# Parallel sliding attention and bilinear GLU on one core: the first weight loads regrouped, one load moved ahead of a transposing DMA, one input load on another queue, the last chunk's logits in one group

## The chip, the cores and the metric

One core of a Trainium2 chip runs the whole kernel. The metric is the device time of one execution in microseconds (us); the runs' median stands for a kernel. Engines are named as in the profile: PE multiplies matrices (PEld loads its weights), DVE works on vectors, ACT applies functions and copies, POOL does small vector work, SP only issues DMAs. ACT and POOL can issue DMAs too.

## What is computed

All tensors are bf16; there are S = 2048 positions of D = 640 numbers, 32 heads of 20, and F = 1536. No layer norm has a gain or bias.

```python
    xn = _layernorm(x)                                   # over the 640 numbers of a position
    q, k, v = split(xn @ wqkv)                           # 32 heads of 20
    idx = pos[:, None] - 2 * arange(8)                   # 8 keys per position: 0, 2, .. 14 back
    logits = where(idx >= 0, einsum("bhsd,bhswd->bhsw", q, k[idx]) * 20 ** -0.5, -1e9)
    o = einsum("bhsw,bhswd->bhsd", softmax(logits), v[idx]) @ wo
    g, u = xn @ w_gate, xn @ w_up
    out = x + o + (g * u) @ w_down
```

## The kernel before

**Tiles and chunks.** The 2048 positions are 16 tiles of 128 positions; four tiles are a chunk of 512 positions, and there are four chunks, 0 to 3. A layer-normed tile is transposed (features on partitions), into `xnT` of its chunk. Tiles 0 to 2 are transposed by PE (L385) and copied by ACT (L390), in the pieces of `PIECES`; tiles 3 to 15 by a transposing DMA that SP issues (L379).

**What a chunk goes through.** `proj` (L500) makes q, k and v of a chunk, 25 matmuls of 128x512 each, evicted by ACT (L504). For chunk 0 it is done in parts, as its tiles come: `proj_tile` (L464, evicted at L477) makes q for tiles 0, 1 and 2 one by one, then `proj` makes k for those three tiles at once, then `proj_tile` makes q and k for tile 3, then `proj` makes v of the chunk. The 8 logits of a position and head are products on DVE (L555), folded there in three steps (L530 twice, L535) and summed over the last numbers of a head by PE with the 0/1 matrix `Ek` (L582) into the PSUM tile `pl`. DVE and ACT make the softmax (L618 the largest, L622, ACT L632 the exponential, L640 the sum, L643 the reciprocal, L649 the result `a`). `a` goes to DRAM (`aD`, L658) and comes back spread over partitions in four DMAs (`aE`, L666). DVE multiplies `aE` with v (L698), adds up in a tree (L708 twice, L706) and has `oT` of a tile. The GLU is 12 steps f of five matmuls with `w_gate` and five with `w_up` (L746), both evicted by ACT (L751), multiplied by DVE into `hT` (L763). Last, `down` multiplies `hT` with `w_down` (L809) and `oT` with `wo` (L812), 34 matmuls of 128x320 a tile, in two halves.

**What sets the order.** Work is a list of steps with engine, cost, dependencies. `Plan.order` places them in a simulated time, on each engine the most urgent of those that are ready, and the instructions are then issued in that order; each engine runs its own in order. `floor` is the planned landing of a load, `PACE` scales the planned cost of DVE's steps, and `GR` says for each chunk in how many groups the logits and the softmax are made; before, chunk 3 has two groups of four matmuls of `pl`, the others one group of eight. The logits' steps are `urgent`: they go first when ready, with a margin of 1 us behind the last fold in the planned time. PE has six banks of PSUM for all else (`ring`), so it can run some steps ahead of ACT's evictions.

**The start (L238 to L240, L879 to L920).** ACT issues three loads for `wq`, of one, two and two of its five blocks of 128 rows (L203), and then x of tile 3 (L179). SP issues x of tiles 0, 1 and 2, then `wk` (L185), then x of tiles 4, 5, 6 and 7, each of which waits for the buffer of the tile five before it (there are five). Then it issues tile 3's transposing DMA, the load of `wv`, and the transposing DMAs of tiles 4 to 7, each behind the layer norm of its tile. Then come `wg`, x of tiles 9 to 12, `wu`, `wd` and `wo`. x of tile 8 is issued by POOL (L412): it needs tile 3's buffer, so it waits for tile 3's transposing DMA, and behind it in POOL's order stand the reciprocal square roots (`rstd`, L267) of tiles 5, 6 and 7, each of which DVE needs to apply the layer norm to its tile (L272). ACT uses x of tile 8 first when it takes the mean of its rows (L326).

Of the kernel before, what the change touches and what calls it, by code (L numbers as in the profile page):

```python
# [9 lines left out]
ACT = mybir.ActivationFunctionType  # L10
# [22 lines left out]
class Plan:  # L33
# [1 line left out]

    LAG = 0.06
    RAW = 0.116
    PACE = {"DVE": 1.03, "ACT": 1.0}
    INORDER = ("DVE", "PE", "ACT")

    def __init__(self):
# [2 lines left out]
    def add(self, eng, cost, fn, deps=(), occ=None, after=(), kb=0):  # L44
        k = self.PACE.get(eng, 1.0)
        s = Step(eng, cost * k, fn, deps, None if occ is None else occ * k, after)
        s.kb = kb
        s.pace = k
        s.idx = len(self.steps)
        self.steps.append(s)  # L50
        return s
# [60 lines left out]
def kernel(  # L112
# [11 lines left out]
    nc = tc.nc  # L124
# [3 lines left out]
    S, D = x_flat.shape  # L128
# [8 lines left out]
    KT = D // P  # L137
    FT = F // P
    NT = S // P
# [16 lines left out]
    wv = const.tile([P, KT, D], BF, name="wv")  # L156
# [10 lines left out]
    add = plan.add  # L167
    T = {}

    def new(key, shape, dtype, tag, bufs, pool=None):  # L170
        t = (pool or sb).tile(shape, dtype, name=tag, tag=tag, bufs=bufs)
        T[key] = t
        return t


    def load_x(t, eng=None):
        def fn():
            x = new(("x", t), [P, D], BF, "x", 5)
            (eng or nc.sync).dma_start(out=x[:], in_=x_flat[t * P : (t + 1) * P, :])  # L179
        return fn  # L180

    X = {}

    def wload(dst, src, eng=None):
        return lambda: (eng or nc.sync).dma_start(out=dst[:], in_=src.rearrange("(i p) f -> p i f", p=P))  # L185
# [10 lines left out]
    def load(at, fn, deps=()):  # L196
        s = chain[0] = add("SP", 2.0, fn, deps, occ=0.45, after=[chain[0]])
        s.floor = at
        return s

    def part(r, lo, hi):
        src = A_wqkv[lo * P : hi * P, r * D : (r + 1) * D].rearrange("(i p) f -> p i f", p=P)
        return lambda: nc.scalar.dma_start(out=WT[r][:, lo:hi, :], in_=src)  # L203
# [29 lines left out]

    C0 = add("POOL", 0.6, consts0)
    WP = []
    for lo, hi, at in ((0, 1, 4.4), (1, 3, 5.1), (3, KT, 5.5)):
        WP.append(add("ACT", at, part(0, lo, hi), [C0], occ=0.48, after=WP[-1:]))
    X[3] = add("ACT", 5.2, load_x(3, nc.scalar), occ=0.45, after=[WP[2]])  # L238
    TB = add("ACT", 1.6, table, after=[X[3]])

    def warm():
# [38 lines left out]
    def behind(s, a):  # L280
        s.after.append(a)
        s.deps.append(a)
        plan.steps.remove(s)
        plan.steps.append(s)
# [5 lines left out]
    def st_in(t, g, d=None):  # L290
        return inline("DVE", 0.48, ln_stats(t, g), [d or X[t]], 0.395)
# [5 lines left out]
    def apply_in(t):  # L297
        XT[t] = inline("DVE", 0.443, ln_apply(t), [RS[t]], 0.4)
# [57 lines left out]
    def pe_main(cost, fn, deps=(), banks=1):  # L356
        nonlocal main
        waits = []
        for k in range(banks):
            if len(ring) + k >= 6:  # L360
                waits.append(ring[len(ring) + k - 6])
        main = add("PE", cost + 0.165, fn, [main, *waits, *deps], occ=cost)
        return main
# [6 lines left out]
    def transposes(t):  # L370
        c, q = divmod(t, CH)

        def slot():
            if q == 0:
                new(("xnT", c), [P, KT, CS], BF, "xnT", XB)

        def dma():
            slot()
            nc.sync.dma_start_transpose(out=T["xnT", c][:, :, q * P : (q + 1) * P], in_=T["x", t][:])  # L379

        def piece(g0, g1, n):
            def pe():
                ps = new(("pst", t, n), [P, KT, P], BF, "ps", 6, psum)
                for g in range(g0, g1):
                    nc.tensor.transpose(ps[:, g, :], T["x", t][:, g * P : (g + 1) * P], ident[:])  # L385

            def ev():
                if n == 0:
                    slot()
                nc.scalar.copy(T["xnT", c][:, g0:g1, q * P : (q + 1) * P], T["pst", t, n][:, g0:g1, :])  # L390
            return pe, ev

        if t in PIECES:
            for n, (g0, g1) in enumerate(PIECES[t]):
                p, e = piece(g0, g1, n)
                w = g1 - g0
                a = pe_main(w * 0.056, p, [XT.get((t, n), XT[t])])
                a = add("ACT", 0.16 + w * P / 1200, e, [a, TT.get(t)], occ=0.07 + w * P / 1200)
                TT[t] = a
                TX.setdefault(t, []).append((g0, g1, a))  # L400
                ring.append(a)
            if t:
                behind(PV[t - 1][0], TT[t])
        else:
            if c < 2:
                a = TT[t] = chain[0] = add("SP", 3.0, dma, [XT[t]], occ=1.28, after=[chain[0]])
            else:
                a = TT[t] = add("SP", 2.8, dma, [XT[t], GP.get(c - XB)], occ=1.28, kb=200)
        if t + 5 < W:
            X[t + 5] = load((11.0, 11.5, 14.2)[t], load_x(t + 5), [a])  # L410
        elif t == 3 or 8 <= t < NT - 5:
            X[t + 5] = add("POOL", 6.0, load_x(t + 5, nc.gpsimd), [a], occ=0.45, kb=160)  # L412

    LL = {}
    GR = (1, 1, 1, 2)
    PV = {}
    R = {}
    PROJ = ("q", "k", "v")
# [12 lines left out]
    def halo(c, r):  # L431
# [10 lines left out]
        else:  # L442
            w = LL.get((c - 2, GR[c - 2] - 1)) if r == 1 else O16.get(CH * (c - 1) - 1)
            HALOCP[r, c] = add("ACT", 0.25, fn, [w, *R[r, c - 1]])

    def lhs(r, i, j):
        return WT[r][:, i, :].rearrange("p (c b) -> p c b", b=KT)[:, :, j]
# [7 lines left out]
    def tile_part(r, t, n, g0, g1, deps):  # L455
        c, q = divmod(t, CH)
        j0, j1 = JS[n]

        def pe():
            if g0 == 0:  # L460
                new(("psv", r, t, n), [P, 512], F32, "ps", 6, psum)
            for j in range(j0, j1):
                for i in range(g0, g1):
                    nc.tensor.matmul(T["psv", r, t, n][:, (j - j0) * P : (j - j0 + 1) * P], lhsT=lhs(r, i, j),  # L464
                                     rhs=T["xnT", c][:, i, q * P : (q + 1) * P], start=(i == 0 and j == j0), stop=(i == KT - 1),
                                     skip_group_check=True)

        ws = WQ[: (1, 2, 2, 3, 3)[g1 - 1]] if r == 0 else WW[r]
        return pe_main((g1 - g0) * (j1 - j0) * 0.056, pe, [*deps, *ws], banks=1 if g0 == 0 else 0)

    def tile_evict(r, t, n, a):
        c, q = divmod(t, CH)
        j0, j1 = JS[n]
        w = j1 - j0

        def ev():
            nc.scalar.copy(where(r, c, j0, j1, q * P, P),  # L477
                           T["psv", r, t, n][:, 0 : w * P].rearrange("p (j s) -> p j s", s=P))

        e = add("ACT", 0.16 + w * P / 1200, ev, [a, HALOCP.get((r, c))], occ=0.07 + w * P / 1200)  # L480
        ring.append(e)
        PV.setdefault(t, []).append(e)
        R.setdefault((r, c), []).append(e)
        TO[e.idx] = q * P
# [8 lines left out]
    def proj(c, r, lo=0, n=CS):  # L493
        for j in range(KT):
# [11 lines left out]
            ts = range(c * CH + lo // P, c * CH + (lo + n) // P)  # L506
            old = LL.get((c - 2, GR[c - 2] - 1)) if r < 2 else O16.get(CH * (c - 1) - 1)
            a = pe_main(KT * (n / 2400 + 0.0027), pe, [*WW[r], *[TT[t] for t in ts], old])
# [55 lines left out]
    before = {}  # L564
    order = [(c, g) for c in range(NCH) for g in range(GR[c])]
    for a, b in zip(order, order[1:]):
        before[b] = a

    def logits(c, g):
        n = (c, g)  # L570
        E = CS // 4 // GR[c]

        def lg():
            if g == 0:
                new(("lps", c), [P, 2 * CS], F32, "pl", 1, psum)
            l = T["lps", c][:, g * W * E : (g + 1) * W * E].rearrange("p (w s) -> p w s", w=W)
            sets = 3 - GR[c]
            for b in range(sets):
# [5 lines left out]

        took = 0.2 + 0.2195 * 2 / GR[c]
        folds = [FO[4 * c + u] for u in range(4) if GR[c] == 1 or u // 2 == g]
# [282 lines left out]
    WQ = WP  # L869
# [6 lines left out]
    halo(0, 1)  # L876
    halo(0, 2)
    transposes(0)
    a0 = [None, None]  # L879
    for k, (g0, g1, x) in enumerate(TX[0]):  # L880
        for n in range(2):
            if k == 2 and n == 1:
                a = st_in(2, 0, None)
                a = st_in(2, 1, a)
                apply_in(1)
                transposes(1)
                WV = None
            a0[n] = tile_part(0, 0, n, g0, g1, [x])
            if k == 2:
                tile_evict(0, 0, n, a0[n])  # L890
# [8 lines left out]
    proj_tile(0, 2, (0,))  # L899
    apply_in(3)  # L900
    transposes(3)
    WV = load(14.6, wload(wv, A_wqkv[:, 2 * D : 3 * D]))
    WW = (WP, [WK], [WV])
    proj_tile(0, 2, (1,))
    proj(0, 1, 0, 3 * P)
# [5 lines left out]
        ln(t)  # L911
        transposes(t)
    WL["g"] = load(28.5, wload(wg, B_w_gate))
    for t in range(9, 13):
        X[t] = load(30.0, load_x(t), [TT[t - 5]])
    WL["u"] = load(36.0, wload(wu, B_w_up))
    proj(0, 2)
# [68 lines left out]
```

## Time and profile before

| | us |
|---|---|
| median of 3 runs (257.4, 257.65, 259.34) | 257.65 |
| the profiled execution | 258.23 |
| its span, first to last instruction | 256.5 |
| PE busy, in 1481 matmuls | 251.8 (98%) |
| DVE busy, in 273 instructions | 223.5 (87%) |
| ACT busy, in 250 instructions | 129.1 (50%) |
| POOL busy, in 61 instructions | 41.8 (16%) |
| DMA, mean of the span | 96 GB/s |
| TensorE clock granted | 1.0 in all stages |

The chain of waits is the way back from the last instruction: at each step to what released it, or to the instruction before it on its engine. A line of the timeline has the start, the time that the group covers, engine, line, operation, tiles and count; in brackets stands the idle time before it and what ended it. The view of DMA issues names for each issuing line the engine, the count, the size of each and the median time from issue to landing; it can be asked for a stretch, so that a single DMA is seen. SPq and ACTq are the parts of SP and ACT that issue and wait. Matmuls overlap, so busy times and ends of single ones are somewhat longer than their distance.

### The profile page before, as it was taken

What the parts mean: (1) busy time and instruction counts of PE and PEld (TensorE: products, weight loads), DVE (VectorE), ACT (ScalarE), POOL (GpSimd) and SP (SyncE); (2) the same over time, 40 slices, a digit from 0 to 9 for tenths busy, and PEclk for the clock granted to TensorE, in tenths of its full rate; (3) what the DMA queues carried; (4) which work ended last, traced back from release to release, by engine and by line L of the source; (5) the groups of instructions that cost most, each with busy time, mean ns of one, the idle gap of its engine ahead of it and who ended that gap; (6) DMA issues with size and microseconds to landing.
All of it is one profiled execution on the core that took longest, in us unless ns stands there. A gap on an engine that the chain in (4) does not pass through costs nothing.

```text
span 256.5 us, 3786 instructions
## 1 busy us (share of the span) xinstructions
PE 251.8 (98%) x1481; PEld 141.4 (55%) x1481; DVE 223.5 (87%) x273; ACT 129.1 (50%) x250; POOL 41.8 (16%) x61
## 2 busy tenths in 40 slices
PE   7999999999999999999999999999999999999995
PEld 2885554444456775444455766444457754445763
DVE  5769999997999999999999999799999999994011
ACT  2656689786589164655554114545542135554100
POOL 2432000411100711004100112000293120000110
PEclk9999999999999999999999999999999999999999
DMA  6895999058500278051400132520005534000221
GB/s 216 259 192 105 399 391 335 3 152 179 157 0 3 27 95 85 7 191 44 170 0 0 17 38 27 145 88 0 0 3 127 130 31 102 23 0 3 24 27 51
DMA packets 21953, 24.65 MB, mean 96 GB/s; under 512 B 10032, under 2 KB 18352, under 8 KB 21872
## 3 DMA queue, kind: packets, MB, share of 16 engines
q1 hardware_dynamic: 18672, 17.86, 24.0%
q0 software_dynamic: 2432, 5.57, 13.5%
q10 hardware_dynamic: 832, 0.98, 1.2%
q8 instruction: 11, 0.18, 0.3%
q14 instruction: 6, 0.05, 0.1%
HBM read 18.61 MB, written 5.96 MB: 96 GB/s over the span
## 4 chain that ended last, share of the span: by engine, by line
PE 96%; DMA 2%; ACTq 0%; DVE 0%; issue 0%
PE ps L746 40%; PE ps L500 23%; PE ps L809 20%; PE ps L812 8%; PE ps L464 3%; DMA wq<-in_A_wqkv_dram 2%; PE pl L582 1%; ACTq L203 0%; PE ps L385 0%; DVE x L820 0%; DVE gs L214 0%; DVE mhalf L216 0%; DVE dm L189 0%
## 5 line engine op out<-in xcount | busy, mean ns | idle before, releaser
L746 PE MATMUL ps<-xnT,wg 128*128 128x512 bf16 x240 | 59.7, 379 | 0.0
L746 PE MATMUL ps<-xnT,wu 128*128 128x512 bf16 x240 | 59.6, 379 | 0.0
L809 PE MATMUL ps<-wd,hT 128*128 128x320 bf16 (+2 forms) x384 | 57.4, 299 | 0.0
L698 DVE TENSOR_TENSOR av<-v,aE 128x5120 bf16<-128x5120 bf16 (+1 forms) x20 | 45.6, 2286 | 3.7 <-DMA aE<-aD 3.7
L809 PEld LDWEIGHTS <-hT 128*128 128x128 bf16 x384 | 37.0, 98 | 16.3 <-issue 0.7
L555 DVE TENSOR_TENSOR pw<-qk 128x2560 bf16<-128x2560 bf16 x28 | 40.8, 1485 | 0.1
L746 PEld LDWEIGHTS <-wu 128*128 128x128 bf16 x240 | 23.5, 98 | 28.3
L746 PEld LDWEIGHTS <-wg 128*128 128x128 bf16 x240 | 23.3, 98 | 28.1 <-issue 0.5
L751 ACT CAST us<-ps 128x512 bf16<-128x512 f32 x48 | 28.1, 585 | 21.2 <-PE ps L746 20.2
L751 ACT CAST gs<-ps 128x512 bf16<-128x512 f32 x48 | 28.1, 585 | 20.4 <-PE ps L746 20.3
L708 DVE TENSOR_TENSOR av<-av 128x2560 bf16<-128x2560 bf16 (+1 forms) x32 | 36.9, 1153 | 0.2
L824 ACT COPY y<-ps 128x320 f32<-128x320 f32 x28 | 11.5, 426 | 42.6 <-PE ps L812 32.7
L853 POOL DMA_DIRECT2D out_dram<-y x14 | 12.2, 871 | 105.3 <-ACT y L824 86.7
L812 PE MATMUL ps<-wo,oT 128*128 128x320 bf16 (+2 forms) x160 | 27.0, 299 | 0.0
L504 ACT CAST qk<-ps 128x512 bf16<-128x512 f32 (+1 forms) x35 | 19.9, 569 | 12.2 <-PE ps L500 12.2
L530 DVE TENSOR_TENSOR pw<-pw 128x2048 bf16<-128x2048 bf16 (+1 forms) x28 | 25.6, 951 | 0.0
L500 PE MATMUL ps<-xnT,wv 128*128 128x512 bf16 x100 | 22.3, 379 | 0.0
L763 DVE TENSOR_TENSOR hT<-gs,us 128x512 bf16<-128x512 bf16 x48 | 19.7, 417 | 2.5 <-ACT us L751 2.3
L500 PE MATMUL ps<-xnT,wk 128*128 128x512 bf16 (+1 forms) x100 | 20.9, 366 | 0.0
L812 PEld LDWEIGHTS <-oT 128*128 128x128 bf16 x160 | 15.5, 98 | 6.3
L790 POOL COPY gate<-hT 1x1 bf16<-1x1 bf16 x4 | 10.6, 2652 | 51.2 <-DVE hT L763 51.2
L500 PEld LDWEIGHTS <-wv 128*128 128x128 bf16 x100 | 11.6, 118 | 9.7 <-issue 0.4
(67 smaller groups left out, 200.8 us busy)
## 6 DMA issues: line engine op xcount, KB each, us to landing
aE<-aD SPq DMA_DIRECT2D x12, 256.0 KB, 4.0
out_dram<-y POOLq DMA_DIRECT2D x14, 160.0 KB, 3.8
wg<-in_B_w_gate_dram SPq DMA_DIRECT2D x1, 1920.0 KB, 9.1
wu<-in_B_w_up_dram SPq DMA_DIRECT2D x1, 1920.0 KB, 13.0
wd<-in_B_w_down_dram SPq DMA_DIRECT2D x1, 1920.0 KB, 17.9
out_dram<-in_A_x_dram POOLq DMA_DIRECT2D x3, 640.0 KB, 4.2
x<-in_A_x_dram SPq DMA_DIRECT2D x11, 160.0 KB, 5.3
aE<-aD SPq DMA_DIRECT2D x8, 128.0 KB, 2.6
```

The source lines that it names most:

```text
L500: nc.tensor.matmul(T[key][:, 0:n], lhsT=lhs(r, i, j), rhs=T["xnT", c][:, i, lo : lo + n], start=(i == 0), stop=(i == KT - 1))
L504: nc.scalar.copy(where(r, c, j, j + 1, lo, n)[:, 0, :], T[key][:, 0:n])
L530: nc.vector.tensor_tensor(w[:, :, lo:hi, :], w[:, :, lo:hi, :], w[:, :, a:b, :], ALU.add)
L555: nc.vector.tensor_tensor(o, qh, kh, ALU.mult)
L698: nc.vector.tensor_tensor(o, v, w, ALU.mult)
L708: nc.vector.tensor_tensor(v[:, 0:k], v[:, 0:k], v[:, k : 2 * k], ALU.add)
L746: nc.tensor.matmul(ps[:], lhsT=(wu if r else wg)[:, i, f * P : (f + 1) * P], rhs=T["xnT", c][:, i, :], start=(i == 0), stop=(i == KT - 1))
L751: nc.scalar.copy(s[:], T[key][:])
L763: nc.vector.tensor_tensor(h[:], T["gs", c, f][:], T["us", c, f][:], ALU.mult)
L809: nc.tensor.matmul(ps, lhsT=T["hT", c, f][:, q * P : (q + 1) * P], rhs=wd[:, f, sl], start=(f == 0), stop=(f == FT - 1 and not wo_part))
L812: nc.tensor.matmul(ps, lhsT=T["oT", t][:, g, :], rhs=wo[:, g, sl], start=False, stop=(g == KT - 1 and f1 == FT))
L853: nc.gpsimd.dma_start(out=out_flat[t * P : (t + 1) * P, :], in_=T["y", t][:], accum_op=ALU.add)
```

## The change

`wq` is loaded in two DMAs, of three and two blocks, in place of three. `wv` is loaded by SP one step earlier: it stood behind tile 3's transposing DMA and stands now between the x of tile 6 and the x of tile 7. The x of tile 8 is issued by SP, after `wg` and with the x of tiles 9 to 12, and no longer by POOL. Chunk 3's logits and softmax are one group of eight matmuls, like those of the other chunks. Three planned landings and DVE's planned pace (1.03 to 1.02) are changed too.

```diff
-    PACE = {"DVE": 1.03, "ACT": 1.0}
+    PACE = {"DVE": 1.02, "ACT": 1.0}
...
-    for lo, hi, at in ((0, 1, 4.4), (1, 3, 5.1), (3, KT, 5.5)):
+    for lo, hi, at in ((0, 3, 4.6), (3, KT, 5.6)):
         WP.append(add("ACT", at, part(0, lo, hi), [C0], occ=0.48, after=WP[-1:]))
-    X[3] = add("ACT", 5.2, load_x(3, nc.scalar), occ=0.45, after=[WP[2]])
+    X[3] = add("ACT", 5.0, load_x(3, nc.scalar), occ=0.45, after=[WP[1]])
...
-        elif t == 3 or 8 <= t < NT - 5:
+        elif 8 <= t < NT - 5:
             X[t + 5] = add("POOL", 6.0, load_x(t + 5, nc.gpsimd), [a], occ=0.45, kb=160)
...
-    GR = (1, 1, 1, 2)
+    GR = (1, 1, 1, 1)
...
-        ws = WQ[: (1, 2, 2, 3, 3)[g1 - 1]] if r == 0 else WW[r]
+        ws = WQ[: 1 + (g1 > 3)] if r == 0 else WW[r]
...
                 apply_in(1)
                 transposes(1)
-                WV = None
+                WV = load(13.8, wload(wv, A_wqkv[:, 2 * D : 3 * D]))
...
     apply_in(3)
     transposes(3)
-    WV = load(14.6, wload(wv, A_wqkv[:, 2 * D : 3 * D]))
...
-    for t in range(9, 13):
+    for t in range(8, 13):
         X[t] = load(30.0, load_x(t), [TT[t - 5]])
```

The order that the plan makes of it was compared with that of before, engine by engine. PE's instructions stand in the same order up to the middle of chunk 1's `down`; from there chunk 2's eight logits matmuls come half a tile of `down` earlier (12 and 5 matmuls), chunk 3's first four (they stood after the first ten matmuls of chunk 2's GLU) are gone, and all eight of chunk 3 stand two halves of a tile before the place where the second four stood, in chunk 2's `down`. SP issues x of tile 4, 5 and 6, `wv`, x of tile 7, five transposing DMAs (tiles 3 to 7), `wg`, x of tiles 8 to 12, `wu`, `wd`, `wo`. POOL issues no load among the `rstd`. On DVE nothing changes before chunk 0's softmax. From there the order is shifted in places: in chunks 0, 1 and 2 one or several steps of the next chunk's products and folds that stood ahead of the first L698 stand behind the last L706 of the chunk, and chunk 3 has four L698 of 5120 elements where it had eight of 2560, and one set of softmax instructions in place of two.

## The prediction

> **What bounds the kernel now.** I read the page first, then the chain of waits in order of time, then SP's and DVE's timelines, and last the view of DMA issues for single stretches of the start.
>
> ```profile
> PE 251.8 (98%) x1481; PEld 141.4 (55%) x1481; DVE 223.5 (87%) x273; ACT 129.1 (50%) x250; POOL 41.8 (16%) x61
> ...
> PE 96%; DMA 2%; ACTq 0%; DVE 0%; issue 0%
> ```
>
> PE is busy for 98% of the span and is 96% of the chain, so the time is the start of PE's dense work, plus its matmuls, plus any gap put between them. Pieces of the chain (start, length, what):
>
> ```profile
> 2.17 5.82 DMA wq<-in_A_wqkv_dram
> ...
> 16.43 2.79 PE ps L464 x50
> 19.22 21.58 PE ps L500 x100
> ...
> 151.02 0.55 PE pl L582 x8
> 151.56 1.74 PE ps L809 x12
> ...
> 166.15 0.33 PE pl L582 x4
> ...
> 206.49 0.33 PE pl L582 x4
> 206.82 1.74 PE ps L809 x12
> ```
>
> The last load of wq lands at 2.17 + 5.82 = 7.99; from there the chain is PE alone, with no gap, until DVE's last step at 253.65. So the gain can only lie ahead of 8 us or in the few logits lines, while a loss can come wherever a supplier has little slack. Who has little slack? SP's timeline gives the issues, the view of DMA issues (one stretch for each line: 11 to 12.2, 12.2 to 13 with two lines, 14.4 to 14.7, 21 to 22) the time to landing in the last column:
>
> ```profile
> 11.11 1.31 SPq L379 DMA_TRANSPOSE xnT<-x  x1
> 12.48 1.92 SPq L185 DMA_DIRECT2D wv<-in_A_wqkv_dram  x1
> 14.50 8.47 SPq L379 DMA_TRANSPOSE xnT<-x  x4
> ```
>
> ```profile
> xnT<-x SPq DMA_TRANSPOSE x1, 4.4
> ...
> q8 instruction: 1, 0.02, 11.5%
> ...
> wv<-in_A_wqkv_dram SPq DMA_DIRECT2D x1, 800.0 KB, 6.4
> ...
> xnT<-x SPq DMA_TRANSPOSE x1, 5.0
> ...
> xnT<-x SPq DMA_TRANSPOSE x1, 2.6
> ```
>
> Tile 3's transpose lands at 11.11 + 4.4 = 15.5 and PE wants it at 16.27 (first L464 of tile 3 in PE's timeline): 0.75 us of slack. wv lands at 12.48 + 6.4 = 18.9, wanted at 19.06: 0.2. Tile 7's transpose lands at 21.77 + 2.6 = 24.4, wanted at 24.45: 0.1. Tile 4's, issued at 14.50 right behind wv, takes 5.0 and lands 0.6 after wv; tile 7's, with nothing ahead of it, takes 2.6: on SP's queue a transpose waits for the load issued before it.
>
> ```profile
> 17.26 0.45 DVE L272 TENSOR_SCALAR x<-x,mv,rstd 128x640 bf16<-128x640 bf16 x1 [2.18 <-POOL rstd L267]
> ...
> 39.71 1.29 DVE L535 TENSOR_TENSOR qk<-av 128x1024 bf16<-128x1024 bf16 x2
> ...
> 146.20 1.29 DVE L535 TENSOR_TENSOR qk<-pw 128x1024 bf16<-128x1024 bf16 x2
> ...
> 167.03 2.83 DVE L698 TENSOR_TENSOR av<-v,aE 128x5120 bf16<-128x5120 bf16 x1 [2.07 <-DMA aE<-aD]
> ...
> 203.08 1.28 DVE L535 TENSOR_TENSOR qk<-pw 128x1024 bf16<-128x1024 bf16 x2
> ```
>
> DVE loses 2.18 us at 15.1 because POOL's rstd stands behind the x of tile 8. Its folds end at 41.0 for chunk 0 (PE takes the logits from 40.74: no slack), at 147.5 for chunk 2 (151.02: 3.5) and at 204.4 for chunk 3's second group (206.49: 2.1).
>
> **The change part by part.** *wq in two loads.* One issue of 0.48 us goes, so the last load and x of tile 3 can land up to 0.48 earlier; the gain ends at 0.22, because tile 1's transposes on PE (8.40) need the layer norm that DVE ends at 7.69 + 0.43 = 8.12, and PE starts 0.06 after DVE at the first tile (5.74, 5.80). Against it, the first five L464 ran at 6.43, and must now wait for three blocks, which with the old second load landed at 7.2. Five matmuls at 0.056 are 0.28. Bounds -0.22 and +0.3; I take 0, since the two meet in the same stretch.
>
> *wv ahead of tile 3's transpose.* SP can issue wv after the x of tile 6 (issued at 8.87, 0.33 long), so at 9.2 and not 12.48: wv lands well before 19.06. But x of tile 7 and the transpose, issued at 10.4 and 11.1, now stand behind its 800 KB. In the first 13 us the busy slices of the DMA view move 354 to 410 GB/s, so 0.82 MB take 2.1 us. In the stretch from 12.2 to 13 an instruction fetch (q8) takes 11.5% of 16 engines for 0.8 us, which is 1.47 us of one engine; the transpose waits for the slowest engine, and the wv data adds to that. Upper bound: all 2.1 us are added, landing 15.5 + 2.1 = 17.6, PE waits 17.6 + 0.1 - 16.27 = 1.4. Lower bound: wv is done in its own 6.4 us, at 15.6; x of tile 7 takes 0.4 (0.16 MB at the same rate) and the transpose 0.6, as tile 4's behind wv: 16.6, a wait of 0.4; and if the transpose did not queue, 0. I take 1.4, since the row nearest to it is the transpose of before itself, with the same fetch on its engine. The x of tile 7 lands at about 17 and DVE wants it at about 15.8 (17.92 less 2.18); that costs DVE some 1 us of the 2.18 won below.
>
> *x of tile 8 on SP's queue.* POOL's rstd of tile 5 is free at 14.4; DVE is 1 to 2 us earlier, and tile 7's transpose, the folds of chunk 0 and wg with it. That moves nothing by itself, since none of them stalls PE now; it gives the cover that PE is not held at 24.45 and 40.74. The load is one issue of 0.47 on SP behind wg; it takes the place of the x of tile 9, which lands at 31.4, and ACT's mean wants it at 31.6. With PE 1.4 later that is covered; uncovered it would hold ACT's evictions, with six banks between them and PE. Cost 0. wu, one load later, lands near 39.2 and is wanted at 42.5. On SP's queue each step issued between tile 7's transpose and the logits' first store (53.59) shifts by that 0.47; no step there is waited for.
>
> *Chunk 3's logits as one group.* Two groups of four cost PE 0.33 each and 0.11 around each (12 L809 take 1.74 behind them and 1.63 elsewhere): 0.88. A group of eight costs 0.55 + 0.11 = 0.66. Gain 0.22. DVE saves 0.8 us of small softmax steps and 0.6 in L698 (eight of 1.484, four of 2.82), which PE doesn't see. What DVE has to keep is the place. Chunk 2's logits stand one half of a tile earlier (2.31): 148.7, and with the 1.4 from the start 150.1. Folds: before 147.5; a step of 1.13 that stood in DVE's wait of 1.68 us in chunk 0 now stands behind the L698s, and in chunk 1 a product of 1.40 does the same where there was no wait (0.2 of wait comes instead), so they end at 147.5 + 1.1 + 0.2 = 148.8: slack 1.3, kept by the late start. From there the first L698 of chunk 2 follows after two products (2.8), the largest, the difference, product and fold (4.9), sum, reciprocal and result (3.4), and a DMA trip of 7.0 (before: issued 160.04, L698 at 167.03): 18.1, so 166.9. Its four sets and twelve L763 took 192.25 - 167.03 = 25.2; then three products and the folds left, 10.3. Chunk 3's folds end at 202.4. PE wants them at 206.49 - 4.62 (two halves) - 0.44 (the first group gone) + 1.4 = 202.8. Slack 0.4: cost 0. Bounds: with chunk 1's trip of 5.0 (108.03 to 113.0) 2 us of slack; with chunk 0's of 7.9 (53.59 to 61.5) a wait of 0.5.
>
> Behind it, the softmax (7 us with the exponential) and a trip of 5 to 8 put the first L698 of chunk 3 at 215 to 218. The last L763 comes 21.6 after it (sums of the same rows), at 237 to 240; PE needs it 4.1 us into `down` (10 L809, 5 L812, and both again), at 235.1 + 1.2 + 4.1 = 240.4. Tile 15's oT comes 3 us after that and is wanted at 252. Covered. The pace only changes the planned order.
>
> Sum: 0 + 1.4 + 0 - 0.22 = +1.2 us. The profiled execution took 258.23, 1.73 over its span, and the median of the three is 0.58 less: 259.4 against that execution, 258.85 against the median, rounded 258.8.
>
> **The rivals.** *Tile 3's transpose is not held* (its slack of 0.75 and a faster wv suffice, say because the fetch falls elsewhere): only the logits and the start count, 257.65 - 0.22 and 0 to -0.22: 257.3. For it: 15 of 16 engines are free of the fetch. Against it: tile 4's 5.0.
>
> *Chunk 3's logits hold PE.* This is the case beyond +1%: the eight matmuls have to wait for the folds if DVE's first L698 of chunk 2 is later than 167.3. From there each us costs one. At the trip of 7.9 the wait is 0.5, so 259.4; for +1% (260.2) the trip would have to be 9.3, longer than any of the five in this trace, or DVE has to lose as much elsewhere, in front of the 25.2 us block. Price up to 2 us: 260.5.
>
> *PE's clock falls in the gap.* The ten warm-up matmuls of 128x512 take 4.45 us, against 1.08 for each five later: a slow clock, at the start alone; granted clock 1.0 afterwards. If the wait at 16.3 brought it back for as long, about 4.5 us at half speed would cost 2.2 us more: 261. The trace has no gap over 0.35 us after the warm-up to judge by, and behind that one (6.87 to 7.20) the clock stays. [...]
>
> **How the numbers follow.** 1% of the median is 2.6 us, about what a measurement here can tell from no change. Forecast (transpose held for 0.4 to 1.4, start up to 0.3: 257.8 to 259.2): 0.60. Transpose not held (257.0 to 257.6): 0.22. Logits hold PE (259.4 to 260.5): 0.13. Clock (260 to 262): 0.03. None of the cases is 2.6 faster; I leave 0.02 for what I don't see. Slower by over 2.6 are the clock case and half of the logits case: 0.10. Within 1%: 0.88. The range from 257.2 (the middle of the second case) to 260.2 leaves out half of the second case's lower part, the clock case and a part of the third.
>
> **What would show it.** In the timeline of the changed kernel: wv issued near 9.3; tile 3's transpose landing at 17.6 and an idle time of PE of 1.4 ended by xnT near 16.3 (the step is wrong if it lands by 16.2); no idle time of DVE for rstd near 15; the first L464 no earlier than 6.9; no PE wait at the L582 lines; a granted clock of 1.0 around 18 us. The prediction fails if a landing that I read as near to its need (x of tile 8 at ACT, wq's three blocks at PE) holds PE by over 1 us.

## The result, and the profile after

The changed kernel takes 258.43 us (median of 22 runs, 258.09 to 259.31); in the same comparison the kernel before takes 257.45 (22 runs, 257.26 to 259.34). The ratio is 1.003, 95% interval 1.0019 to 1.004, so the change costs 0.5 to 1.0 us. The profiled execution of the changed kernel took 258.12, its span is 256.3.

The page of the changed kernel: busy times, the clock granted to TensorE in 40 slices, and the shares of the chain by engine.

```profile
PE 251.6 (98%) x1481; PEld 141.7 (55%) x1481; DVE 223.5 (87%) x264; ACT 129.0 (50%) x249; POOL 41.4 (16%) x60
...
PEclk9999999999999999999999999999999999999999
...
PE 93%; DMA 3%; DVE 3%; POOL 0%; issue 0%
```

No engine has over 0.3 us more to do than before (PEld 141.7 us, before 141.4), and the clock granted is 1.0 from its first record in the trace, at 7.08, to PE's last matmul. The chain is 93% PE where it was 96%: the first 16 us of it have moved to other engines. Its pieces in the changed kernel (start, length, what):

```profile
9.13 0.07 issue
9.20 0.56 POOL rstd L267
9.76 0.03 issue
9.78 0.46 DVE x L272
10.24 0.02 issue
10.25 5.77 DMA xnT<-x
16.03 0.05 issue
16.07 2.99 PE ps L464 x50
...
148.46 0.54 PE pl L582 x8
149.00 1.74 PE ps L809 x12
...
201.19 0.54 PE pl L582 x8
201.73 1.74 PE ps L809 x12
```

PE's work now starts, for the chain, at 16.07, when tile 3's transposing DMA has landed; before, it was PE alone from 8 us on. The three logits pieces (0.55, 0.33 and 0.33) are two of 0.54, and neither has a wait. The idle time itself in PE's timeline and in that of its weight loads, same kernel:

```profile
16.07 1.59 PE L464 MATMUL ps<-xnT,wq 128*128 128x128 bf16 x25 [0.26 <-DMA xnT<-x]
```

```profile
16.07 1.44 PEld L464 LDWEIGHTS <-wq 128*128 128x128 bf16 x25 [0.63 <-DMA xnT<-x]
```

The two differ by 0.37, since the profile models the ends of matmuls; below I go by starts. SP's timeline and single stretches of the view of DMA issues (10.2 to 10.3, then 9.6 to 10) of the changed kernel give the cause:

```profile
8.63 0.43 SPq L185 DMA_DIRECT2D wv<-in_A_wqkv_dram  x1
9.77 0.33 SPq L179 DMA_DIRECT2D x<-in_A_x_dram  x1
10.25 10.26 SPq L379 DMA_TRANSPOSE xnT<-x  x5
```

```profile
xnT<-x SPq DMA_TRANSPOSE x1, 5.8
...
x<-in_A_x_dram SPq DMA_DIRECT2D x1, 160.0 KB, 5.7
```

wv is issued at 8.63 (before: 12.48), and what stands behind it is slow: x of tile 7 takes 5.7 us (before: 4.5), the transpose 5.8 (4.4). DVE's timeline of the changed kernel, next to the row of 2.18 us that the prediction showed:

```profile
15.46 0.89 DVE L253 BATCH_NORM_STATS2 st<-x 128x6 f32<-128x320 bf16 x2 [0.46 <-DMA x<-in_A_x_dram]
...
164.59 2.83 DVE L698 TENSOR_TENSOR av<-v,aE 128x5120 bf16<-128x5120 bf16 x1 [0.23 <-DMA aE<-aD]
...
198.98 1.29 DVE L535 TENSOR_TENSOR qk<-pw 128x1024 bf16<-128x1024 bf16 x2
```

The 2.18 us behind POOL's rstd are gone, 0.46 for x of tile 7 came. Chunk 3's last fold ends at 200.27 and PE takes the logits at 201.12: they fit, by 0.85.

### The profile page after: what moved, and what is told of

Its sections match the earlier page's. It is cut to its first block, busy times and chain, and to the rows that moved or that the text cites. A ratio compares the mean times of both kernels' runs of the same rounds, so it can differ in the third digit from the quotient of the medians.

```text
span 256.3 us, 3767 instructions
## 1 busy us (share of the span) xinstructions
PE 251.6 (98%) x1481; PEld 141.7 (55%) x1481; DVE 223.5 (87%) x264; ACT 129.0 (50%) x249; POOL 41.4 (16%) x60
## 4 chain that ended last, share of the span: by engine, by line
PE 93%; DMA 3%; DVE 3%; POOL 0%; issue 0%
PE ps L746 40%; PE ps L500 21%; PE ps L809 20%; PE ps L812 8%; DMA xnT<-x 2%; DVE st L253 1%; PE ps L464 1%; DMA x<-in_A_x_dram 1%; PE pl L582 1%; DVE x L272 1%; DVE ve L261 0%; DVE mv L259 0%; POOL rstd L267 0%; DVE x L820 0%
## 5 line engine op out<-in xcount | busy, mean ns | idle before, releaser
L809 PE MATMUL ps<-wd,hT 128*128 128x320 bf16 (+2 forms) x384 | 57.4, 299 | 0.0
L698 DVE TENSOR_TENSOR av<-v,aE 128x5120 bf16<-128x5120 bf16 x16 | 45.1, 2820 | 3.9 <-DMA aE<-aD 3.9
L809 PEld LDWEIGHTS <-hT 128*128 128x128 bf16 x384 | 37.0, 98 | 16.5 <-issue 0.8
L853 POOL DMA_DIRECT2D out_dram<-y x14 | 12.2, 872 | 103.8 <-ACT y L824 103.8
L504 ACT CAST qk<-ps 128x512 bf16<-128x512 f32 (+1 forms) x35 | 19.9, 568 | 11.2 <-PE ps L500 11.2
L500 PE MATMUL ps<-xnT,wv 128*128 128x512 bf16 x100 | 22.3, 379 | 0.0
L500 PE MATMUL ps<-xnT,wk 128*128 128x512 bf16 (+1 forms) x100 | 20.9, 366 | 0.0
L500 PEld LDWEIGHTS <-wv 128*128 128x128 bf16 x100 | 11.6, 117 | 9.7 <-issue 0.4
```

Source lines behind the costliest of these rows:

```text
L500: nc.tensor.matmul(T[key][:, 0:n], lhsT=lhs(r, i, j), rhs=T["xnT", c][:, i, lo : lo + n], start=(i == 0), stop=(i == KT - 1))
L504: nc.scalar.copy(where(r, c, j, j + 1, lo, n)[:, 0, :], T[key][:, 0:n])
L698: nc.vector.tensor_tensor(o, v, w, ALU.mult)
L809: nc.tensor.matmul(ps, lhsT=T["hT", c, f][:, q * P : (q + 1) * P], rhs=wd[:, f, sl], start=(f == 0), stop=(f == FT - 1 and not wo_part))
L853: nc.gpsimd.dma_start(out=out_flat[t * P : (t + 1) * P, :], in_=T["y", t][:], accum_op=ALU.add)
```

## A second profile of before

Each kernel below was timed together with the kernel before. The first two are the kernels of this case once more.

> The kernel before, unchanged: a second profile. The profile of before took 258.23 us, 0.8 over its median of 257.45, so its start may have been a slow one: there one DMA engine was about 1 us behind the other fifteen from 4.5 us on, and wq's last load landed at 7.99. If the late engine belongs to that one execution, a second profile has wq's last load at about 6.8 and a span near 255.6; if it belongs to the kernel, it is there again at 8.0. Ratio 1.000.

> The changed kernel, unchanged: a second profile. The one at hand took 258.12 us, near its fastest (258.09) and 0.3 under its median. If tile 3's transposing DMA behind wv is the loss, PE's wait for xnT is 0.4 us in the fast profile and 0.6 to 1.0 in one near the median, and there is no other gap. Ratio 1.003.

before_again: 257.45 us (257.27 to 258.67), ratio to the other runs of before 0.9986 [0.9965, 1.0007]. after_again: 258.38 (258.03 to 258.91), ratio 1.0014 [0.9995, 1.0033]. The chain of before_again shows that the start which the prediction read was not the usual one:

```profile
1.28 4.43 PE ps L244 x10
5.71 0.69 PE ps L385 x5
6.39 0.28 PE ps L464 x5
6.68 0.01 issue
6.69 1.05 PE ps L464 x16
...
15.61 2.79 PE ps L464 x50
18.40 5.61 PE ps L500 x26
```

There is no wait for wq in it: PE is dense from its first warm-up matmul on. In the profile of before that the prediction used, one DMA engine was late: a packet of 1280 bytes took 1.1 us at 4.46, and wq's last load landed at 7.99; here it lands at 6.67. So 0.8 us of that execution's span were its own start. Tile 3's transpose takes 4.1 us here, lands at 14.46, and PE comes to it at 15.44: 1.0 us of slack. (The last line of the fence ends where the view did; the piece goes on.)

From here on "later" means: the start of the same matmul against before_again. PE in the changed kernel's first profile is 0.63 later at tile 3's first L464 (16.07), 0.45 behind chunk 3's logits (206.29 against 205.84), and its span is 0.76 longer (256.30, 255.54). In after_again the three numbers are 0.86, 0.68 and 1.01. So there are three terms: about +0.6 to +0.9 at the transpose, -0.18 from the logits, and +0.3 after PE's last matmul, which the prediction did not have. PE's own idle time at the transpose is less than 0.63 in the first profile: PE was 0.21 later already at its first L500 (11.59 against 11.38), because its first L464 ran slower (6.17 to 7.78, against 6.24 to 7.58), and the wait for the landing takes these 0.21 in. In after_again PE was not late there (11.36).

## Experiments on wv, the transpose and x of tile 8

**wv ahead, nothing else**, on the kernel before:

```diff
-                WV = None
+                WV = load(13.8, wload(wv, A_wqkv[:, 2 * D : 3 * D]))
...
-    WV = load(14.6, wload(wv, A_wqkv[:, 2 * D : 3 * D]))
```

> Before, with nothing changed but wv's load, which SP issues ahead of x of tile 7 and tile 3's transposing DMA; the order on PE, DVE, ACT and POOL is that of before. Theory of the queue: tile 3's transpose lands 0.5 to 2 us later than in before, PE waits 0.4 to 1.4 us for xnT at 16 us, and the time is 0.6 to 1.4 us over before (ratio 1.002 to 1.005). Rival, the loss comes from the later order (chunk 3's logits as one group and the order that it brings): ratio 1.000, wait under 0.2 us.

258.89 us (258.63 to 259.86), ratio 1.0034 [1.0015, 1.0053]. More than the whole change. PE's, ACT's, DVE's and POOL's timelines of this kernel, in that order:

```profile
16.12 1.59 PE L464 MATMUL ps<-xnT,wq 128*128 128x128 bf16 x25 [0.24 <-DMA xnT<-x]
...
24.95 5.56 PE L500 MATMUL ps<-xnT,wq 128*128 128x512 bf16 x25 [0.45 <-ACT v L504]
```

```profile
21.47 0.75 ACT L477 CAST qk<-ps 128x384 bf16<-128x384 f32 x2 [3.35 <-DVE pw L555]
```

```profile
17.77 0.45 DVE L272 TENSOR_SCALAR x<-x,mv,rstd 128x640 bf16<-128x640 bf16 x1 [3.38 <-POOL rstd L267]
```

```profile
16.38 0.76 POOL L179 DMA_DIRECT2D x<-in_A_x_dram  x1 [3.59 <-DMA xnT<-x]
17.16 0.57 POOL L267 TENSOR_TENSOR rstd<-ve,mhalf 128x1 f32<-128x1 f32 x1
```

Read from the last fence upward: POOL's load of x of tile 8 waits for the transpose, now 1.6 later; the rstd behind it is later; DVE waits 3.38 for it and comes late to its first products; an eviction of ACT waits 3.35 for one of these; and PE waits a second time at 24.95, 0.45 us for an eviction of ACT's (L504). PE is 0.67 later at the first wait, 0.71 behind it, 1.32 at the second and 1.43 from chunk 0's logits to the end. The next run takes the load off POOL.

**wv ahead and x of tile 8 on SP**, on the kernel before:

```diff
-                WV = None
+                WV = load(13.8, wload(wv, A_wqkv[:, 2 * D : 3 * D]))
...
-    WV = load(14.6, wload(wv, A_wqkv[:, 2 * D : 3 * D]))
...
-        elif t == 3 or 8 <= t < NT - 5:
+        elif 8 <= t < NT - 5:
...
-    for t in range(9, 13):
+    for t in range(8, 13):
```

> The kernel before, with wv ahead of x of tile 7 and of tile 3's transpose, and x of tile 8 on SP's queue. Theory: with wv ahead alone PE waited twice, 0.24 and more for xnT near 16.1 (0.67 us later than before by then) and 0.45 for the evictions of v at 24.95 (1.3 to 1.4 us later behind it); the second wait came from POOL's load of x of tile 8, which waits for tile 3's transpose and holds the rstd of tiles 5 to 7. With that load on SP the second wait is gone: tile 3's transpose lands near 16.1, PE is 0.6 to 0.9 later from there to the end, 258.1 to 258.3 us. Rival: the wait at 24.95 comes from DMA work that is late in any case: it is there again, PE 1.3 to 1.5 later, 258.9.

258.3 us (257.82 to 259.22), ratio 1.0026 [1.0014, 1.0039]. PE's timeline:

```profile
17.11 1.59 PE L464 MATMUL ps<-xnT,wq 128*128 128x128 bf16 x25 [0.27 <-DMA xnT<-x]
...
25.33 4.91 PE L500 MATMUL ps<-xnT,wq 128*128 128x512 bf16 x22
```

The first wait is there, the second is gone, as the theory says. Its size can't be checked in this profile: the execution began 1.2 late, with a wait of 0.98 for wq; the transpose adds 0.47 to that, where 0.6 to 0.9 was expected, and PE is 1.67 later at the transpose and 1.70 behind it.

**x of tile 8 on SP, nothing else** (the last two pairs of lines of that diff):

> The kernel before, with x of tile 8 on SP's queue and nothing else. Theory: DVE's idle time for rstd near 15 goes and DVE is 1 to 2 us earlier there, but PE waits for nothing at that place, so PE's matmuls stand where they stood to 0.1 us and the time is 257.3 to 257.6. Rival: x of tile 8 comes late for ACT's mean (near 31.6), ACT's evictions are held and PE loses 0.3 or more around 32: 257.8 or above.

257.7 us (257.23 to 258.72), ratio 0.9999 [0.9985, 1.0013]. No gain and no loss by itself. DVE waits for no rstd near 15, and the theory's "to 0.1 us" for PE's starts could not be read off: this execution lost 0.6 at its start, where wk landed late (6.4 us where before_again has 5.0).

**The changed kernel with wv behind the transpose again** (the wv lines of the diff turned back):

> The changed kernel with wv's load put back behind tile 3's transposing DMA; the order on the other engines is that of the changed kernel. Theory of the queue: the loss goes, 0.6 to 1.4 us less than the changed kernel, and as the start and the logits gain up to 0.5, it stands at 0.998 to 1.000 of before; wv lands at about 18 to 19 and is wanted at about 18.6, so up to 0.4 us can come back as a wait for wv. Rival (later order): 1.003, as the changed kernel.

257.54 us (257.44 to 258.15), ratio 0.998 [0.996, 1.0]. The place of wv carries the loss: 0.84 us between the medians of after_again and of this kernel, timed together. Its profiled execution has no wait for xnT. (That one is the longest of its runs, 258.15: PE is 0.64 later from 8.22 on, where it waits 0.29 for the layer norm of tile 1.)

**Queue or bandwidth?** In the kernel before, POOL issues wv, behind tile 3's rstd, so on another queue than the transposes:

```diff
-    WV = load(14.6, wload(wv, A_wqkv[:, 2 * D : 3 * D]))
+    WV = add("POOL", 5.0, wload(wv, A_wqkv[:, 2 * D : 3 * D], nc.gpsimd), [RS[3]], occ=1.0)
```

> The kernel before, with the load of wv issued by POOL behind tile 3's rstd, so about when SP issued it with wv ahead, but on another queue than the transposes. Theory A, order within SP's queue: the transpose has only x of tile 7 ahead of it and lands by 15.2, PE waits 0.2 or less at tile 3's first L464, and the time is within 0.3 of before (257.2 to 257.7). Theory B, shared bandwidth: wv's 800 KB take the engines' time whatever the queue, the transpose lands at 15.7 or later, PE waits 0.4 or more, 258.0 to 258.4.

259.11 us (258.54 to 260.07, 6 runs), ratio 1.0056 [1.0037, 1.0075]. The view of DMA issues for 9.7 to 10.2 and for 10.2 to 10.6, then PE's timeline:

```profile
wv<-in_A_wqkv_dram POOLq DMA_DIRECT2D x1, 800.0 KB, 6.3
x<-in_A_x_dram SPq DMA_DIRECT2D x1, 160.0 KB, 2.3
```

```profile
xnT<-x SPq DMA_TRANSPOSE x1, 6.2
```

```profile
16.57 1.59 PE L464 MATMUL ps<-xnT,wq 128*128 128x128 bf16 x25 [0.79 <-DMA xnT<-x]
```

Theory A falls: on a queue of its own the transpose takes 6.2 us and PE waits longer. So a place behind wv in the same queue is not needed to make it slow. Theory B fits: in the trace the transpose's packets of 256 bytes start at 12.80, and wv's packets on POOL's queue run from 11.64 to wv's landing at 16.0, so the two move at the same time; how the DMA engines divide themselves between them is not shown. x of tile 7 took 2.3 us here, but that doesn't tell what the queue does to a plain load: its last packet of 1280 bytes starts at 11.54, ahead of wv's first. The median is 0.7 above what theory B allowed and the profiled execution was this kernel's fastest; where the other runs lose the rest is open. The plan's order is also changed in places here. POOL's load of x of tile 8 waits for the transpose as in only_wv (to 16.82), but DVE has one layer norm less ahead of its first product, ACT waits 1.73 in place of 3.35, and PE not at all: the second wait of only_wv takes the late load and that kernel's order together.

## Experiments on wq, the logits and the end

**wq in two loads, nothing else** (the wq and x of tile 3 lines of the change):

> The kernel before, with wq in two loads and nothing else. Theory: PE is dense from its warm-up on, so nothing at the start can gain: the same to 0.1 us up to the end, where the last store is on another semaphore (some 0.05 later): 257.4 to 257.6. Rival 1: the saved issue lets x of tile 3 and wq's last blocks land earlier and PE's stretch before 8.5 us shortens by 0.2: 257.2. Rival 2: the first L464 wait for three blocks: 0.1 to 0.3 later, 257.6 to 257.8.

257.62 us (257.31 to 258.09), ratio 0.9996 [0.9987, 1.0005]; PE's starts are within 0.1 of before_again from the warm-up to the end, but for chunk 0's logits, which the plan now puts five matmuls later. The theory holds: no gain to be had where PE is dense.

**Chunk 3's logits in one group, with the pace, nothing else:**

```diff
-    PACE = {"DVE": 1.03, "ACT": 1.0}
+    PACE = {"DVE": 1.02, "ACT": 1.0}
...
-    GR = (1, 1, 1, 2)
+    GR = (1, 1, 1, 1)
```

> Before with chunk 3's logits as one group and DVE's planned pace of the changed kernel; wq, wv and x of tile 8 as in before. By the offsets of PE's matmuls in the two profiles of the changed kernel, PE gains 0.2 us from the one group of eight. By their last 2 us, the end costs 0.3 more: the store that lands last is on a semaphore that SP waits for second in its closing list, and the rest of the list is walked after it; with five DMAs fewer the last store falls on that same semaphore here. Theory: +0.1 us, 257.4 to 257.7, ratio 1.000, PE's last matmul 0.2 earlier than in before, no wait of PE at the logits. Rival (the later order holds PE or the group is dearer): 258 or more with a wait of PE behind 100 us.

257.96 us (257.32 to 259.48), ratio 1.0008 [0.999, 1.0027]: as a total not to be told from no change, though the median is 0.3 above what the theory allowed. The profiled execution is this kernel's longest one (259.48, span 257.8), and it shows the rival that ends above 259. Its PE timeline, then DVE's:

```profile
201.31 0.39 PE L582 MATMUL pl<-qk,Ek 128*32 128x512 bf16 x2
202.20 0.40 PE L582 MATMUL pl<-qk,Ek 128*32 128x512 bf16 x4 [0.50 <-DVE qk L535]
202.81 0.39 PE L582 MATMUL pl<-qk,Ek 128*32 128x512 bf16 x2 [0.20 <-DVE qk L535]
```

```profile
167.07 2.82 DVE L698 TENSOR_TENSOR av<-v,aE 128x5120 bf16<-128x5120 bf16 x1 [2.31 <-DMA aE<-aD]
...
201.47 1.29 DVE L535 TENSOR_TENSOR qk<-pw 128x1024 bf16<-128x1024 bf16 x2
```

DVE's first L698 of chunk 2 waits 2.31 for its data, is at 167.07 where the changed kernel has 164.59, and everything behind it moves: the folds end at 202.76, PE wants them from 201.31 on, and is 1.5 us later behind these logits than ahead of them (in the changed kernel 0.2). PE had lost 0.5 already in chunk 2's `down`, waiting twice for an `hT` of DVE's (L809 at 190.66 and 193.87). The difference is the trip through DRAM: 159.40 to 167.07, so 7.67 us, against 159.00 to 164.59, 5.59, in the changed kernel. It begins with the store of `a`; the view of DMA issues for 158.7 to 159.8, the changed kernel and then only_gr:

```profile
aD<-a SPq DMA_DIRECT2D x1, 256.0 KB, 2.3
```

```profile
aD<-a SPq DMA_DIRECT2D x1, 256.0 KB, 3.8
```

The long trip is not an accident of this execution. POOL stores a finished tile (L853, 160 KB) at about the same time. In the changed kernel that store is issued at 159.10, just behind the store of `a`; in only_gr at 158.81, ahead of it, and the store of `a` lands (163.22) only when that one has (163.05). In the nine profiles in which POOL's store is 0.6 to 0.7 us ahead, the store of `a` takes 3.4 to 3.8 us and chunk 2's trip 6.2 to 8.2; in the five in which it is behind, or ahead by 0.09, they are 2.2 to 2.8 and 5.3 to 5.7. These five are the profiles of the changed kernel and of its variants. No run moves this one store alone, so the cause is argued, not shown.

**The last 0.3 us.** The program's closing lines have SP wait for the semaphores of its DMAs, one by one in a fixed order. Views of waits of SP, before_again and the changed kernel:

```profile
SPq L981 <- DMA out_dram<-x: 0.7, 2, 0.5
```

```profile
SPq L980 <- DMA out_dram<-x: 1.1, 1, 1.1
```

In the trace the loads and stores take their semaphores in turn, out of eight, so the number of DMAs that SP and ACT issue decides which one the last store gets. Numbered as the list comes to the eight, before ends on the sixth, with few waits behind the landing; the changed kernel has five such DMAs fewer in all (57, before 62), its last store has the first, and SP waits there and then walks the rest. From the last landing to the end: 1.04 us before, 1.35 after. Adding DMAs of one column of x (256 bytes) that nobody reads, in the middle of the kernel, moves it:

```diff
+    def extra(k):
+        def fn():
+            z = sb.tile([P, 1], BF, name=f"z{k}", tag=f"z{k}")
+            nc.sync.dma_start(out=z[:], in_=x_flat[0:P, k : k + 1])
+        return fn
+    z = AE[1, 0, 3]
+    for k in range(3):
+        z = add("SP", 2.0, extra(k), [O16[CH + 1]], occ=0.5, after=[z])
```

Three on the kernel before (so that it ends as the changed one does), five on the changed kernel (so that it ends as the one before does):

> Before with three more DMAs of 256 bytes, which SP issues between chunk 1's and chunk 2's spreads, where its queue is idle; nothing else changes, on any engine. Eight semaphores are given to SP's and ACT's DMAs in turn, so the last store moves from the sixth to the first of them. Theory of the end: SP waits for it second in its closing list, and walks some eight waits of 0.06 us after it where three were left: the time grows by 0.3 us (257.75, ratio 1.0012) and the end behind PE's last matmul by 0.3. Rival (the end's 0.3 comes from something else in the changed kernel): 257.45, no change at the end.

> The changed kernel with five such DMAs more, so that the last store falls on the same semaphore as in before. Theory of the end: 0.3 us less than the changed kernel, 258.1 (ratio 1.0025), with the wait for xnT at 16 us as before. Rival: 258.4.

before_3_dma_more: 257.94 us (257.68 to 260.27), ratio 1.0017 [0.9992, 1.0041]; PE at most 0.06 later from 7 us on, 1.35 from the last landing to the end. after_5_dma_more: 258.01 (257.76 to 258.33), ratio 1.0011 [0.9998, 1.0024]; PE 0.46 later at the end, span 0.46 longer, 1.05 from landing to end. The views of waits show the two exchanged:

```profile
SPq L991 <- DMA out_dram<-x: 1.1, 1, 1.1
```

```profile
SPq L990 <- DMA out_dram<-x: 0.8, 2, 0.5
```

The totals alone do not settle 0.3 us (both intervals take in 1); the landings do, and over all profiles the stretch goes by the place in the list: 1.34 to 1.35 on the first (five profiles), 1.10 and 1.11 on the fifth (two), 1.04 to 1.05 on the sixth (four), 0.98 on the seventh (two), 0.92 on the eighth (one).

**The changed kernel with wv back and seven such DMAs**, so that the last store has the eighth:

> The changed kernel with wv's load back behind tile 3's transposing DMA and seven small DMAs more, so that the last store falls on the semaphore that stands last in SP's closing list. If wv alone costs the wait and the list the end, this beats both kernels: the logits' 0.2 and 0.1 more at the end than before, 257.1 (ratio 0.9988 to 0.9992). Rival: the small DMAs or the order cost something too, 257.5.

257.26 us (256.99 to 257.87), ratio 0.9985 [0.9971, 0.9999]. PE waits for nothing at the transpose (its L464 run at 15.63 without idle time) nor at the logits. It is ahead of both kernels: by 0.01 to 0.29% of the one before, and its median is 0.75 us below that of after_5_dma_more, timed together, and 1.2 below the changed kernel's, which was not.

## Why the prediction was right or wrong

The forecast of +1.2 us met +0.98 (medians). The mechanism was right, but two terms were off in opposite directions, 0.5 to 0.8 too much at the transpose and 0.3 too little at the end, so part of the closeness is luck.

*wq in two loads: right, 0.* Shown by only_wq. The reason given (two effects that meet) was not the right one. The wait for three blocks did not come: they land at 5.39 in the changed kernel, and the first L464 runs at 6.17, where the prediction's sign said no earlier than 6.9. Nor was there a gap to close in the usual start: PE waits for wq in five of the fourteen profiles, and in each of them the last of that load's 16 completions is 0.6 to 1.2 us late. One of these waits is the one that the prediction named: in after_5_dma_more the load of three blocks lands at 6.46, and the first L464 runs at 6.51 and not 6.2. The wait for the transpose then covers it. "The gain can only lie ahead of 8 us" read the 7.99 of one execution as the kernel's.

*wv ahead of the transpose: mechanism right, size off.* The step "I take 1.4" failed: 0.63 and 0.86 were measured. By the prediction's own sign ("wrong if it lands by 16.2") the first profile speaks against the step, with a landing at 16.03, and after_again, with 16.26, only just for it; but the sign's times are those of the execution that began 0.8 late. "All 2.1 us are added" became 1.6 (landing 14.46 to 16.03), and the slack was 1.0, not 0.75, in the execution that did not begin late. With that execution's times the same upper bound would have been 1.2. The value lies inside the bounds of 0.4 and 1.4. The cause given, "on SP's queue a transpose waits for the load issued before it", is not enough: wv_from_POOL has the same delay from another queue. The rival "transpose not held" is out.

*x of tile 8 on SP: right, and worth more than it seemed.* Nothing alone (only_x8), but it is the cover: without it wv ahead costs a second wait of 0.6 at 24.95 (only_wv), and with it that wait is gone (wv_and_x8). The prediction named that place (24.45) and gave the uncovered case no price. Its 31.4 for the landing of x of tile 9 is in no row: in the profile of before that load is issued at 23.69, takes 8.9 and lands at 32.6, too late for ACT's mean at 31.6. In the changed kernel x of tile 8 lands at 30.1 and ACT takes it at 31.45, because SP comes to wg 2.4 us earlier (20.57, before 23.02).

*Chunk 3's logits: right.* -0.18 for -0.22, folds ahead by 0.85, in after_again by 0.50, for the 0.4 forecast. The rival with its point at 167.3 was real: only_gr loses PE time at a first L698 of 167.07, with a trip of 7.67; PE is 1.5 us later behind the logits than ahead of them, and 0.5 went ahead of that. (The trip of 9.3 that the prediction gives for +1% does not follow from its own numbers: from 259.4 at a trip of 7.9, one us each, it is 8.7.) In the changed kernel's profile both things help, a short trip (5.59) and a PE that is 0.63 later; in wv_back_7_dma_more PE isn't late, the trip is 5.34, and the folds fit with no wait.

*The end: the missing term, +0.3.* "Sum" took what lies behind PE's last matmul as unchanged. It depends on the number of DMAs.

*The clock: right.* Gaps of up to 1 us (0.98 in wv_and_x8) left the granted clock at 1.0: the five L385 that follow that gap take 0.44, as in before. A wait of 1.4, as forecast, did not come, so what it would do to the clock is not shown. The slow clock at the start can be seen in the changed kernel: its first L464 stand 0.11 apart (6.26 to 7.01), those from 7.17 on 0.055, and the record of a granted clock of 1.0 begins at 7.08.

Sum by the profiles: 0.63 - 0.18 + 0.31 = 0.76, the spans say 0.76; with after_again 0.86 - 0.18 + 0.31 = 0.99, the spans say 1.01.

## What to carry to other kernels

Before a large load is moved ahead of a small transfer that PE will wait for, compare the small one's slack with what the load can add to its time (here 1.0 us, and 1.6 for 800 KB); another queue did not help here (a transpose of 6.2 us in wv_from_POOL), a later issue did (no wait for xnT in after_wv_back). Take two profiles of the kernel before, because a start with one late DMA engine lengthens an execution by as much as such a change is worth (0.8 us here). When a move delays one transfer, ask which engine has an instruction waiting for it: here a load on POOL turned a delay of 1.6 us into a second wait three engines away. Before a kernel's end is taken as fixed, count the DMAs: five fewer cost 0.3 us here.

## What the runs showed of the hardware

- Behind the last landing, SP's closing waits cost some 0.06 us each (in the changed kernel eight end from 255.00 to 255.43): 0.92 to 1.35 us by the place of the last store's semaphore, which the count of DMAs before it decides.
- At the start of some executions one of a load's 16 completions was over 1 us late, and PE went on only behind it. In the first profile of before, fifteen of wq's last load were in at 6.78 and the last at 7.99 (a packet of 1280 bytes took 1.1 us), and PE took it at 8.03; in wv_and_x8 the last of wq's second load came 1.1 us behind the others, with a PE wait of 0.98, and in only_x8 the last of wk 1.5. In six of the fourteen profiles some load of the first 9 us has its last completion over 1 us behind the fifteenth. It is a likely part of the spread of the runs (257.26 to 259.34 for one kernel), which only the profiled ones let one see.
- A transposing DMA of 128x640 with an 800 KB load issued 0.6 to 2.0 us ahead took 5.5 to 6.2 us, on the load's own queue and on another; without it 3.6 to 4.4 at the same place.
- The 256 KB store of the softmax's result landed after 2.2 to 2.8 us, or after 3.4 to 3.8 where a 160 KB store on POOL's queue had been issued 0.6 to 0.7 us ahead of it; the trip through DRAM that it begins took 5.3 to 5.7 or 6.2 to 8.2.
